# Float64 weights clamped on GpSimd one piece ahead, and VectorE's side work placed on other steps

## The chip, the cores and the metric

One core of a Trainium2 chip runs the whole kernel as one program. The metric is the device time of one execution in microseconds. Three executions of the kernel before took 1365.23, 1365.89 and 1360.34 us; their median is 1365.23 us. A profiled execution took 1369.21 us, of which the profile's span shows 1367.3 us.

## The reference

Three blocks follow each other. First attention of 8 batches and 8 heads over 576 positions of width 64, in two stages: 32 packed queries `p` attend to `k` and `v`, and then `q` attends to the packed result. Second a dense layer on the 4608 tokens (512 wide), whose weights are float64 in memory:

```python
h = x @ w_in            # 512 -> 2048
g = h - np.tanh(h)
x = (g @ w_out).astype(np.float32)   # 2048 -> 512
```

Third a mixture of 8 experts with one expert for each token, chosen by the largest gate logit: `out = gate_w * eom * (relu(x @ w1[e]) @ w2[e])`.

## The kernel before, in words

**The stages.** Stage A (context `pa`, 0 to about 128 us) packs `p` with `k` and `v` in 16 units `u` of one batch and four heads. The main stage (context `pb`, to about 860 us) does the second attention stage and the dense layer, and chooses the experts. Then come the experts. The change touches stage A and the main stage.

**Main stage.** The work goes in 16 halves `i`, each of half a batch (288 tokens, `HN`), numbered `(b, hf)`: an even half has `hf` = 0, an odd one 1. A half has 16 steps `f`, one for each 128 of the 2048 inner columns. Loop body number `m` issues, in this order: `up_b(m+1)`, `up(m+2)`, `down(m)`, at the last step of a half `drain`, and then what the table `todo` holds for this half and step, in the order in which `at` put it there. Each engine works in the order of issue.

- `up` (12 matmuls, L504 to L506) makes `ph` from the attention weights `a_hi`, `a_lo` of q and from the batch's fused weights `wf_hi`, `wf_lo`; ScalarE makes `th`, VectorE `gg = ph - th` (L510).
- `up_b` splits `gg`: ScalarE makes `gh` (L517), and `gl = gg - gh` (L518) is GpSimd's for the first `GP` = 12 steps of half 0 and VectorE's elsewhere.
- `down` (12 matmuls, L530 to L532) needs `gh` and `gl`, and adds to four accumulators in PSUM. Tiles `gg`, `gh`, `gl` and `ph` have two buffers each.
- `drain` copies the accumulators to `x2s` (one buffer), on ScalarE and VectorE (L540).

**The side work of the main stage**, put on steps by hand with `at`:

- `attend(i, fs, b, hf)`: the attention weights of one half. `load_q` (16 DMAs on SP into `qt`, two buffers) stands three steps before the first of `fs`; then `att_q` (VectorE transpose L175), `att_s` (16 matmuls L182 into two `px` banks), `att_f` (VectorE reads these), `att_x`, `att_n`, `att_t` (makes `a_hi`), `att_l` (makes `a_lo`). `up` of the next half's first step is issued in step 14.
- `weave(i, f, c, n)`: a quarter of the next batch's fused weights. `fuse` (16 matmuls L220 into two `px` banks) in step `f`, `fuse_h` (ScalarE) and `fuse_l` (VectorE `wf_lo`, L228, twice) in step `f` + 1.
- `make_z(n)`: 16 VectorE transposes of 32x32 (L159) of the next batch's packed result, in even halves. `fuse` and `att_s` read `z`.
- For the half before: `logits`, `logits_b`, `choose_a`, `choose_b`, `rank` (two matmuls into a `px` bank), `place` (VectorE, reads this bank at L597 and L601, then three indirect DMAs of GpSimd), `gate`, `gate_b` (VectorE, its multiply is L631; then four DMAs of `x2s` to DRAM on SP).

`px` is a pool of two PSUM banks that `att_s`, `fuse`, `logits`, `logits_b` and `rank` share.

**The conversion of the float64 weights.** `plan` lists 32 pieces of 128x512 numbers: 0 to 15 are of `w_in`, 16 to 31 of `w_out`. The first 20 (`NA`) are converted in stage A, one or two for each unit, and one in each of the steps 0 to 11 of half 0. `load_ahead(done)` keeps three pieces (`NST` buffers `st`) asked for on SP. `narrow` makes float32 out of a piece's two 32-bit words `hi` and `lo`: ScalarE takes the magnitude (L105), VectorE shifts and merges the bits (L107, L108, L109) and compares the magnitude with `TINY` (L110), and GpSimd multiplies by that mask (L113), which makes zeros of the smallest numbers. For `w_out`, `part_out` splits the piece one step later: ScalarE makes `hi` (L136), GpSimd `lo` (L137). In stage A a unit issues, near its end: `pack`'s reciprocal (L296, L297), the exponential (L277), `part_out` of the last unit's pieces, the conversion, and `load_ahead`.

## Time and profile before

| | us |
|---|---|
| median of three runs | 1365.23 |
| the profiled execution | 1369.21 |
| its span in the profile | 1367.3 |
| busy: TensorE, VectorE, ScalarE, GpSimd | 1265.3, 816.1, 530.1, 327.9 |

Busy times of the engines lie beside each other and don't add up to the span. In rows of the profile PE is TensorE (PEld its weight loads), DVE VectorE, ACT ScalarE, POOL GpSimd, SP the queue that issues most DMAs; L108 is line 108 of the kernel. A row of a timeline has the start in us from the span's start, the duration in us and the instruction; instructions of one line that follow each other are merged (x16), and in brackets stands the idle time of the engine before it and what ended it. Matmul ends are modelled.

### The profile page before, as it was taken

To read this page: it belongs to the slowest core of one execution; us is meant where nothing else is said; L and a number is where in the kernel's file an instruction comes from. 1 tells how busy PE (TensorE), PEld (TensorE's weight loads), DVE (VectorE), ACT (ScalarE), POOL (GpSimd) and SP (SyncE) were. 2 spreads that over 40 slices of the span, in tenths; PEclk is the share of its full clock that TensorE was granted. 3 is DMA by queue.
4 is the path that set the end of the run, shared out by engine and by line. 5 is a ranking of instruction groups with operands and counts; after the bars stand their busy time and mean duration, and the time that the engine had idled before them with its cause. 6 is when DMAs were issued, how large, how long until landed. Compare 5 with 4: busy or idle time off the path is not lost. (4 is left out here: it accounts for less than half of the span.)

```text
span 1367.3 us, 25742 instructions
## 1 busy us (share of the span) xinstructions
PE 1265.3 (93%) x9024; PEld 1082.4 (79%) x9024; DVE 816.1 (60%) x1811; ACT 530.1 (39%) x1141; POOL 327.9 (24%) x363
## 2 busy tenths in 40 slices
PE   6575879999999999999999999869999999999997
PEld 5354668998989989889899899757888778788775
DVE  3755996777776777768677777363233533443551
ACT  4555434443434344343434435332222422332431
POOL 3313760000000000000000000115444444454431
PEclk7878889999999999999999999989999999999999
DMA  8999421122111221122103023331113311332441
GB/s 227 242 246 207 138 64 22 15 36 36 27 19 27 36 30 24 19 36 36 26 11 53 19 47 112 117 80 39 44 47 101 105 46 45 113 100 73 131 154 41
DMA packets 140354, 102.24 MB, mean 75 GB/s; under 512 B 97296, under 2 KB 121876, under 8 KB 139572
## 3 DMA queue, kind: packets, MB, share of 16 engines
q1 hardware_dynamic: 130516, 80.33, 25.5%
q0 software_dynamic: 9696, 20.14, 4.8%
q8 instruction: 74, 1.21, 0.4%
q14 instruction: 68, 0.56, 0.2%
HBM read 215.60 MB, written 19.57 MB: 172 GB/s over the span
## 5 line engine op out<-in xcount | busy, mean ns | idle before, releaser
L610 POOL DMA_INDIRECT tab<-tok,ix x48 | 45.3, 943 | 641.5 <-DVE ix L608 460.7
L517 ACT ACTIVATE gh<-gg 128x288 fp32r<-128x288 f32 x256 | 112.6, 440 | 153.2 <-PE acc L532 68.0
L518 DVE TENSOR_TENSOR gl<-gg,gh 128x288 fp32r<-128x288 f32 x244 | 109.9, 450 | 96.9 <-ACT gh L517 90.6
L531 PE MATMUL acc<-gl,wo_bt 128*128 128x288 f32 x512 | 154.9, 303 | 11.5 <-DVE gl L518 7.0
L851 DVE TENSOR_TENSOR hl<-pt,hh 128x512 fp32r<-128x512 f32 x76 | 52.3, 690 | 185.4 <-ACT hh L850 174.2
L504 PE MATMUL ph<-a_hi,wf_hi 128*128 128x288 f32 x512 | 160.5, 314 | 0.9 <-DVE gg L510 0.5
L506 PE MATMUL ph<-a_hi,wf_lo 128*128 128x288 f32 x512 | 152.7, 298 | 3.9 <-DVE wf_lo L228 3.9
L531 PE MATMUL acc<-gl,wo_a 128*128 128x288 f32 x512 | 152.8, 298 | 3.7 <-POOL gl L518 3.7
L795 POOL DMA_INDIRECT xg<-x2d,iq x132 | 138.4, 1049 | 64.5 <-issue 57.0
L530 PE MATMUL acc<-gh,wo_a 128*128 128x288 f32 x512 | 152.1, 297 | 1.8 <-ACT pp L298 1.8
L532 PE MATMUL acc<-gh,wo_bt 128*128 128x288 f32 x512 | 152.8, 298 | 0.0
L530 PE MATMUL acc<-gh,wo_bt 128*128 128x288 f32 x512 | 152.7, 298 | 0.0
L505 PE MATMUL ph<-a_lo,wf_hi 128*128 128x288 f32 x512 | 152.3, 297 | 0.0
L532 PE MATMUL acc<-gh,wo_a 128*128 128x288 f32 x512 | 152.3, 297 | 0.0
L510 DVE TENSOR_TENSOR gg<-ph,th 128x288 f32<-128x288 f32 x256 | 115.9, 453 | 55.6 <-ACT th L508 54.3
L839 ACT ACTIVATE h<-ph 128x512 f32<-128x512 f32 x76 | 45.3, 598 | 241.1 <-PE ph L838 205.3
L508 ACT ACTIVATE th<-ph 128x288 f32<-128x288 f32 x256 | 104.1, 406 | 78.8 <-PE ph L506 77.7
L504 PEld LDWEIGHTS ph<-a_hi,wf_hi 128*128 128x128 f32 x512 | 97.3, 190 | 43.4 <-issue 38.6
L860 PE MATMUL py<-w2h,hh 128*128 128x512 f32 x304 | 127.0, 418 | 0.2
L861 PE MATMUL py<-w2l,hh 128*128 128x512 f32 x304 | 121.1, 398 | 1.7 <-DVE w2l L765 1.7
L837 PE MATMUL ph<-w1l,xh 128*128 128x512 f32 x304 | 121.2, 399 | 1.4 <-DVE w1l L765 1.0
L862 PE MATMUL py<-w2h,hl 128*128 128x512 f32 x304 | 120.8, 397 | 0.0
(223 smaller groups left out, 2756.8 us busy)
## 6 DMA issues: line engine op xcount, KB each, us to landing
raw<-in_moe_w_dram SPq DMA_DIRECT2D x37, 2048.0 KB
sraw<-in_moe_w_dram SPq DMA_DIRECT2D x37, 1024.0 KB
x2s<-in_moe_w_dram SPq DMA_DIRECT2D x37, 1024.0 KB
kt<-in_k_dram SPq DMA_DIRECT2D x16, 576.0 KB
vt<-in_v_dram SPq DMA_DIRECT2D x48, 192.0 KB
x2d<-x2s SPq DMA_DIRECT2D x64, 144.0 KB
qt<-in_q_dram SPq DMA_DIRECT2D x240, 36.0 KB
st<-in_moe_w_in_dram SPq DMA_DIRECT2D x16, 512.0 KB
```

The lines of the kernel that those rows point to most:

```text
L504: pe.matmul(ph, lhsT=wf_hi[n][:, g, c], rhs=ah[:, g], start=g == 0, stop=False)
L505: pe.matmul(ph, lhsT=wf_hi[n][:, g, c], rhs=al[:, g], start=False, stop=False)
L506: pe.matmul(ph, lhsT=wf_lo[n][:, g, c], rhs=ah[:, g], start=False, stop=g == 1)
L510: vec.tensor_tensor(gg, ph, th, op=ALU.subtract)
L530: pe.matmul(acc[j], lhsT=hi[:, j], rhs=gh, start=f == 0, stop=False)
L531: pe.matmul(acc[j], lhsT=hi[:, j], rhs=gl, start=False, stop=False)
L532: pe.matmul(acc[j], lhsT=lo[:, j], rhs=gh, start=False, stop=f == NF - 1)
L795: pool.indirect_dma_start(xg[:, g], None, src, bass.IndirectOffsetOnAxis(ap=iq[:, g:g + 1].bitcast(U32), axis=0))
L837: pe.matmul(ph, lhsT=xh[:, c], rhs=w1l[:, c, r], start=False, stop=False)
L860: pe.matmul(py, lhsT=hh[:, c], rhs=w2h[:, c], start=c == 0, stop=False)
L861: pe.matmul(py, lhsT=hh[:, c], rhs=w2l[:, c], start=False, stop=False)
L862: pe.matmul(py, lhsT=hl[:, c], rhs=w2h[:, c], start=False, stop=c == 7)
```

## The change

Conversion: the mask goes. `clamp` takes the magnitude of `hi` as float32 on ScalarE and raises it to at least `TINY` on GpSimd (one source, in place); VectorE's three bit operations then start from the clamped tile, and the last writes the result. `convert` clamps the next piece right after it has converted one, if that piece is asked for. `cvt` gets a third buffer. `lo` of `part_out` and the first 12 `gl` go from GpSimd to VectorE.

Main stage: `make_z` is cut by head over the steps 1, 3, 6 and 13. The even halves' `attend` ends in step 12 instead of 11; the odd halves' `att_q` goes from step 5 to 1 (with `load_q` from step 2 to step 14 of the half before). The fuses go from the steps 2, 5, 9, 14 to 3, 9, 11, 14. `rank`, `place`, `gate`, `gate_b` go from 4, 5, 5, 6 to 5, 6, 5, 7 in odd halves and to 4, 5, 6, 9 in even ones; halves 14 and 15 keep theirs.

```diff
--- before.py
+++ after.py
@@ -33,12 +33,11 @@
 NSTEP = NMAIN + NTAIL
 TROWS = NE * CAP + 128
 PAD = NT
-TINY = 1.125 * 2.0 ** -15
+TINY = 2.0 ** -15
 HF = NF // 2
 NST = 3
 UNITS = 2 * NB
 NA = 20
-GP = 12
 
 
 @with_exitstack
@@ -98,20 +97,34 @@
         return t[:, f % HF, 0], t[:, f % HF, 1]
 
 
-    def narrow(dst, st):
+    clamped = {}
+
+    def clamp(st):
+        t = cv.tile([128, 512], I32, name="cvt", bufs=3)
+        act.activation(t.bitcast(F32), st[:, :, 1].bitcast(F32), AF.Abs)
+        pool.tensor_scalar(t.bitcast(F32), t.bitcast(F32), TINY, None, op0=ALU.max)
+        return t
+
+    def narrow(dst, st, t):
         hi, lo = st[:, :, 1], st[:, :, 0]
-        top = st.rearrange("p n w -> p (n w)").bitcast(BF16).rearrange("p (n w) -> p n w", w=4)[:, :, 3]
-        mag = cv.tile([128, 512], BF16, name="mag")
-        act.activation(mag, top, AF.Abs)
-        t = cv.tile([128, 512], I32, name="cvt")
-        vec.tensor_scalar(t, hi, 0x07FFFFFF, 3, op0=ALU.bitwise_and, op1=ALU.logical_shift_left)
+        vec.tensor_scalar(t, t, 0x07FFFFFF, 3, op0=ALU.bitwise_and, op1=ALU.logical_shift_left)
         vec.scalar_tensor_tensor(t, lo, 29, t, op0=ALU.logical_shift_right, op1=ALU.bitwise_or)
-        vec.scalar_tensor_tensor(t, hi, -0x40000000, t, op0=ALU.bitwise_and, op1=ALU.bitwise_or)
-        vec.tensor_scalar(mag, mag, TINY, None, op0=ALU.is_ge)
-        src = t.bitcast(F32)
-        dst = src if dst is None else dst
-        pool.tensor_tensor(dst, src, mag, op=ALU.mult)
-        return dst
+        dst = t if dst is None else dst.bitcast(I32)
+        vec.scalar_tensor_tensor(dst, hi, -0x40000000, t, op0=ALU.bitwise_and, op1=ALU.bitwise_or)
+        return dst.bitcast(F32)
+
+    def clamp_next(i):
+        if i < len(plan) and i < ahead[0] and i not in clamped:
+            _, conv, n = plan[i]
+            st, w = (wst, w_out) if conv is conv_out else (ist, w_in)
+            if w.dtype != F32:
+                clamped[i] = clamp(st[n])
+
+    def convert(i):
+        _, conv, n = plan[i]
+        clamp_next(i)
+        conv(n, clamped.pop(i, None))
+        clamp_next(i + 1)
 
     wst, ist = {}, {}
 
@@ -124,17 +137,17 @@
             wst[f] = cv.tile([128, DM, 2], I32, name="st", bufs=NST)
             sp.dma_start(wst[f].rearrange("p n w -> p (n w)"), rows.bitcast(I32))
 
-    def conv_out(f):
+    def conv_out(f, t):
         wf = wst.pop(f)
         if w_out.dtype != F32:
-            wf = narrow(None, wf)
+            wf = narrow(None, wf, t)
         wst[f] = wf
 
     def part_out(f):
         sv = wst.pop(f).rearrange("p (g j d) -> p j g d", g=4, j=4)
         hi, lo = (x.rearrange("p j (g d) -> p j g d", g=4) for x in wo_of(f))
         act.activation(hi, sv, AF.Copy)
-        pool.tensor_tensor(lo, sv, hi, op=ALU.subtract)
+        vec.tensor_tensor(lo, sv, hi, op=ALU.subtract)
 
     def load_w_in(n):
         m, j = divmod(n, 4)
@@ -145,15 +158,17 @@
             ist[n] = cv.tile([128, 512, 2], I32, name="st", bufs=NST)
             sp.dma_start(ist[n].rearrange("p n w -> p (n w)"), w_in[rows, cols].bitcast(I32))
 
-    def conv_in(n):
+    def conv_in(n, t):
         m, j = divmod(n, 4)
         if w_in.dtype != F32:
-            narrow(w_in_sb[:, j, 512 * m:512 * m + 512], ist.pop(n))
-
-    def make_z(b):
-        z = z_t[b] = ef.tile([128, 4, 32], F32, name="zt", bufs=2)
+            narrow(w_in_sb[:, j, 512 * m:512 * m + 512], ist.pop(n), t)
+
+    def make_z(b, hs=range(4)):
+        if b not in z_t:
+            z_t[b] = ef.tile([128, 4, 32], F32, name="zt", bufs=2)
+        z = z_t[b]
         for g in range(2):
-            for h in range(4):
+            for h in hs:
                 for e in range(2):
                     r = 64 * (h % 2) + 32 * e
                     vec.transpose(z[r:r + 32, 2 * g + h // 2], pp[32 * h:32 * h + 32, 2 * b + g, 32 * e:32 * e + 32])
@@ -461,8 +476,8 @@
                 part_out(n)
             late = []
             want = (NA * u + LA - 2) // (LA - 1)
-            for _, conv, n in plan[done:want]:
-                conv(n)
+            for x, (_, conv, n) in enumerate(plan[done:want]):
+                convert(done + x)
                 if conv is conv_out:
                     late.append(n)
             done = want
@@ -515,7 +530,7 @@
             gh = gp.tile([128, HN], F32R, name="gh")
             gl = gp.tile([128, HN], F32R, name="gl")
             act.activation(gh, gg, AF.Copy)
-            (pool if (b, hf) == (0, 0) and f < GP else vec).tensor_tensor(gl, gg, gh, op=ALU.subtract)
+            vec.tensor_tensor(gl, gg, gh, op=ALU.subtract)
             g_t[b, hf, f] = gh, gl
 
         acc = {}
@@ -659,10 +674,11 @@
                 at(i, 1, logits_b)
                 at(i, 2, choose_a)
                 at(i, 3, choose_b)
-                at(i, 4, rank)
-                at(i, 5, place, *p_)
-                at(i, 5, gate, *p_)
-                at(i, 6, gate_b, *p_)
+                r, p_at, g_at, gb_at = (4, 5, 5, 6) if i >= 14 else (5, 6, 5, 7) if i % 2 else (4, 5, 6, 9)
+                at(i, r, rank)
+                at(i, p_at, place, *p_)
+                at(i, g_at, gate, *p_)
+                at(i, gb_at, gate_b, *p_)
             if i == 0:
                 weave(0, 0, 1, 0)
                 weave(0, 4, 2, 0)
@@ -676,7 +692,7 @@
                     part = []
                     take = plan[done:done + (2 if len(plan) - done > NF - 3 - f else 1)]
                     for x, (_, conv, m) in enumerate(take):
-                        at(0, f, conv, m)
+                        at(0, f, convert, done + x)
                         if conv is conv_out:
                             part.append(m)
                             assert f + 1 < m
@@ -688,15 +704,16 @@
             if n == NB:
                 continue
             if hf == 0:
-                attend(i, (4, 6, 7, 8, 9, 10, 11), b, 1)
-                at(i, 12, make_z, n)
+                attend(i, (4, 6, 7, 8, 10, 11, 12), b, 1)
+                for h, f in enumerate((1, 3, 6, 13)):
+                    at(i, f, make_z, n, (h,))
             else:
-                attend(i, (5, 7, 8, 9, 10, 11, 12), n, 0)
+                attend(i, (1, 7, 8, 9, 10, 11, 12), n, 0)
                 if n == NB - 1:
                     attend(i, (8, 12, 13, 14, 15, 16, 17), n, 1)
-                weave(i, 2, 0, n)
-                weave(i, 5, 1, n)
-                weave(i, 9, 2, n)
+                weave(i, 3, 0, n)
+                weave(i, 9, 1, n)
+                weave(i, 11, 2, n)
                 weave(i, 14, 3, n)
 
 
```

## Rows read from the trace of the kernel before

**Rows 1.** the page's first section, the whole span: busy time of each engine

```profile
PE 1265.3 (93%) x9024; PEld 1082.4 (79%) x9024; DVE 816.1 (60%) x1811; ACT 530.1 (39%) x1141; POOL 327.9 (24%) x363
```

**Rows 2.** windows: us of the stretch, then busy us (instructions) of each engine, PEclk, DMA share, GB/s

```profile
0.00:128.00 128.00, 81.63 (x1239) 60.00 (x1240) 66.67 (x161) 67.77 (x153) 32.65 (x60) 0.80 1.01 238
140.00:200.00 60.00, 46.37 (x294) 38.66 (x279) 59.00 (x84) 25.39 (x55) 42.86 (x35) 0.85 0.40 108
208.00:860.00 652.00, 644.03 (x5115) 585.84 (x5114) 471.66 (x1238) 272.88 (x667) 42.50 (x45) 1.00 0.20 33
```

**Rows 3.** waits of TensorE, the whole run: us in total, times, longest

```profile
PE pk L256 <- DMA kt<-in_k_dram: 28.1, 11, 6.5
```

**Rows 4.** groups by line and form, VectorE, 139.95 to 199.1 us: busy us, mean ns, idle

```profile
L108 DVE SCALAR_TENSOR_TENSOR cvt<-st,cvt 128x512 int32<-128x512 int32 x12 | 15.4, 1287 | 0.4
L109 DVE SCALAR_TENSOR_TENSOR cvt<-st,cvt 128x512 int32<-128x512 int32 x12 | 14.1, 1176 | 0.4
L107 DVE TENSOR_SCALAR cvt<-st 128x512 int32<-128x512 int32 x12 | 9.3, 774 | 0.0
...
L110 DVE TENSOR_SCALAR mag<-mag 128x512 bf16<-128x512 bf16 x13 | 4.8, 366 | 0.0
...
L518 DVE TENSOR_TENSOR gl<-gg,gh 128x288 fp32r<-128x288 f32 x2 | 0.9, 448 | 0.0
```

**Rows 5.** timeline, 149 to 156 us: start us, us, engine and instruction

```profile
151.03 1.72 POOL L137 TENSOR_TENSOR wo_a<-cvt,wo_a 128x512 fp32r<-128x512 f32 x1
...
151.65 1.65 DVE L109 SCALAR_TENSOR_TENSOR cvt<-st,cvt 128x512 int32<-128x512 int32 x1
```

**Rows 6.** timeline, VectorE, 108 to 124 us; idle time and its end in brackets

```profile
118.52 0.43 DVE L107 TENSOR_SCALAR cvt<-st 128x512 int32<-128x512 int32 x1 [3.83 <-DMA st<-in_moe_w_out_dram]
...
119.71 0.69 DVE L109 SCALAR_TENSOR_TENSOR cvt<-st,cvt 128x512 int32<-128x512 int32 x1
```

**Rows 7.** groups by line and form, whole run

```profile
L765 DVE TENSOR_TENSOR w1l<-raw,w1h 128x1024 fp32r<-128x1024 f32 x20 | 23.2, 1218 | 1.8 <-ACT w1h L764 1.8
...
L113 POOL TENSOR_TENSOR cvt<-cvt,mag 128x512 f32<-128x512 f32 x16 | 19.0, 1185 | 21.9 <-DVE mag L110 21.4 <-DVE rs L296 0.5
```

**Rows 8.** instructions of line 386: duration ns min/median/max, first and last start us

```profile
L386 POOL COPY scr<-scr x4: 396/494/595, 5.2 to 86.2; 128x256 f32<-128x256 f32 x4
```

**Rows 9.** timeline, TensorE, half 4 (to 384.96 us) and half 5

```profile
361.04 0.72 PE L182 MATMUL px<-qT,zt 64*32 64x288 f32 x16
...
379.33 0.29 PE L530 MATMUL acc<-gh,wo_bt 128*128 128x288 f32 x1
380.20 0.40 PE L531 MATMUL acc<-gl,wo_bt 128*128 128x288 f32 x1 [0.59 <-DVE gl L518]
...
382.56 0.30 PE L530 MATMUL acc<-gh,wo_bt 128*128 128x288 f32 x1
...
401.22 1.50 PE L220 MATMUL px<-w_in_sb,zt 64*32 64x512 f32 x16
...
403.56 0.30 PE L530 MATMUL acc<-gh,wo_a 128*128 128x288 f32 x1
...
405.94 0.29 PE L530 MATMUL acc<-gh,wo_a 128*128 128x288 f32 x1
...
408.03 1.31 PE L182 MATMUL px<-qT,zt 64*32 64x288 f32 x16 [0.33 <-DVE wf_lo L228]
...
414.24 1.09 PE L220 MATMUL px<-w_in_sb,zt 64*32 64x512 f32 x16
```

**Rows 10.** timeline, VectorE, halves 4 and 5

```profile
376.22 3.44 DVE L159 STREAM_TRANSPOSE zt<-pp 32x32 f32<-32x32 f32 x16
...
406.02 1.36 DVE L631 TENSOR_TENSOR x2s<-x2s,gw 128x1152 f32<-128x1152 f32 x1
407.29 1.28 DVE L228 TENSOR_TENSOR wf_lo<-px,wf_hi 128x512 fp32r<-128x512 f32 x2
```

**Rows 11.** timeline, ScalarE, 111 to 119 us

```profile
112.20 0.67 ACT L105 ACTIVATE mag<-st 128x512 bf16<-128x512 bf16 x1
```

## The prediction

> **What bounds the kernel now.** The page comes first: TensorE is busy for 93% of the span, VectorE for 60%, GpSimd for 24% [rows 1]. Averages over unlike stages, so the second view is a table by stage [rows 2]. It shows three regimes that the change touches. From 0 to 128 us (attention, `pa`) the DMA engines are full (share 1.01, 238 GB/s), and the longest wait of TensorE in the whole run is there, 28.1 us for k [rows 3]. From 140 to 200 us, half 0 of the main stage, VectorE is busy for 59.0 of 60 us and TensorE for 46.4, at a granted clock of 0.85 (a mix of the 1.2 and 2.4 GHz levels): VectorE bounds. From 208 to 860 us TensorE is busy for 644.0 of 652 us at clock 1.00 (2.4 GHz), so VectorE (471.7) costs only where something it owes comes late. After 860 us nothing is changed.
>
> **Half 0, the conversion.** Read the VectorE groups of its 12 pieces, plan numbers 20 to 31 [rows 4]: L107 0.774, L108 1.287, L109 1.176, L110 0.366, together 3.60 us a piece. The same instructions with GpSimd idle take 0.43 and 0.69 us [rows 6] (L108 like L109, both 128x512 with two sources). The surplus is waiting: L109 starts 0.62 us behind GpSimd's L137, which lasts 1.72, and takes 1.65 instead of 0.69 us [rows 5]. It ends about its own 0.69 us after GpSimd does.
>
> Removed per piece on VectorE: the four at 3.60. Added: three unheld, 0.43 + 0.69 + 0.69 = 1.81 (L107 now reads a plain tile; I take no gain for that). ScalarE's magnitude stays one instruction of 128x512, 0.67 [rows 11], off the bound. Added from GpSimd: `lo` of `part_out`, 128x512 with two SBUF sources, not in the trace on VectorE; bounds are half of the 1024-column subtract, 0.61 [rows 7], and L109's 0.69. I take 0.61, the same operation. And `gl` of the first 12 steps at 0.45 [rows 4]. Balance: 3.60 - 1.81 - 0.61 - 0.45 = 0.73 us a piece, 12 pieces, 8.8 us gained, before GpSimd's new clamp holds anything.
>
> The clamp, one source, 128x512: the nearest rows are a copy of 256 columns at 0.494 [rows 8], as a floor, and the two-source multiply of 512 columns that it replaces, 1.19 [rows 7], as a ceiling. Twice the copy is 0.99; less some fixed part I take 0.9. The Trainium skill, GPSIMD Engine Reference, Elementwise, counts about 1.8 cycles per element, 0.77 us here, and advises against GpSimd for an elementwise maximum; by 0.77 the held time below would be 4.6 and not 5.4 us. When does it hold VectorE? In a step ScalarE does `gh`, `th`, the `hi` of the previous piece and the next magnitude; VectorE meanwhile does `gl` and `gg`, then `lo` and the conversion. The clamp so arrives about when `lo` or L107 is running and takes its turn. In steps 1, 4, 5, 7, 8 and 9 of half 0 VectorE has pieces there that read PSUM or one tile (`fuse_l`, `att_q`, `att_f`, a reduction, ...), and the clamp runs beside them; in the other six it holds: 6 x 0.9 = 5.4 us. Ends: no step, 0; all twelve at 1.19, 14.3. Half 0 thus gains 3.4 us, between -5.5 and +8.8.
>
> **Stage A and its seam.** The clamp takes L110 off VectorE, which there waits on ScalarE, but loads bound that stage, so I count nothing. Against it: the magnitude is now computed one piece earlier, and ScalarE works in order. The magnitude of piece 15 ended at 112.87, and the next one would stand there, while VectorE's L107 shows that piece 16 landed only at 118.52 [rows 6, 11]. ScalarE would be held 5.6 us with the copies of the next attention unit behind it. Cover: TensorE's 28.1 us of waits for k, which lie in the same stage. At the seam VectorE loses the wait on the magnitude in front of the last unit's reciprocal, and gets four `lo` that wait for `hi`: about even. I take 0, between -3 and +3.
>
> **Main stage, odd halves.** A bare step is 2.38 us (403.56 to 405.94). Two bursts on the `px` banks are stretched [rows 9]. The fuse of step 5 lasts 1.50 against 1.09 of a free one, because its second bank is still `rank`'s until `place` has read it: 0.41. `att_s` in step 7 lasts 1.31 against 0.72 in the even half, and idles 0.33 in front: 0.92. The VectorE rows say why: `gate_b`'s 1.36 us multiply stands ahead of the two `wf_lo` that free the banks [rows 10]. The change moves the fuse of step 5 to 9, and `att_s` of 7 finds the banks long free. Both waits go, 1.33 us. But the fuse of step 9 moves to 11, and its predecessor's `wf_lo` stands in step 10 behind `att_n`, the same figure as step 6 today: one large piece, then `wf_lo`, then a burst one step on. I charge 0.92 for it, between 0 and 1.33. Net 0.41 a half, 7 halves: 2.9 us.
>
> In half 13 the second `attend` is left where it was, so its `att_s` stands in step 12 ahead of the `wf_lo` for the fuse of step 11, whose banks it needs. Nearest row 0.92; more here, as `att_l` is ahead too: 1.3, once.
>
> **Even halves.** `make_z`, 3.44 us in one piece at step 12 [rows 10], delays `gl`: TensorE idles 0.59 in step 14, and the step lasts 3.23 instead of 2.38 [rows 9], 0.85 lost. Six halves have it: 5.1 us. Spread by head, a quarter is 0.86 us, and steps 1, 3, 6, 13 have room. What is late next: `gate_b` now falls in step 9, between `att_x` and `att_n`, and `a_lo` moves from 11 to 12, two steps before the first use. By adding up VectorE's queue, `gl` of steps 12 and 13 comes late by a few tenths. I leave 0.3 of the 0.85, between 0 and 0.85: gain 6 x 0.55 = 3.3 us.
>
> **Moved at no cost.** `load_q` of the odd halves, 16 DMAs on SP, goes from step 2 to step 14 of the half before; it follows `gate_b`'s four writes on SP (then at step 9), and `att_q` comes three steps later; two `qt` buffers cover it. Gone, `att_q` would wait, with `gl` behind it. `gate_b`'s writes at 9 and 7 instead of 6 still leave six steps before `drain` needs their tile. `place` a step later moves three indirect DMAs on GpSimd, which is otherwise idle there (42.5 of 652 us) [rows 2].
>
> **Sum.** 3.4 + 0 + 2.9 - 1.3 + 3.3 = 8.3 us. The profiled execution took 1369.2 us and would take 1360.9; the median of the runs, 1365.2, is 4.0 lower, so I forecast 1357.
>
> **The rivals.** (1) *The lock takes back half 0.* If each clamp holds VectorE, 12 x 0.9 = 10.8 eats the 8.8. For it: L107, L108 and L109 are all held today [rows 4 to 6], and `lo` and `gl` read two tiles as L109 does; against it, half of the steps have other work there. If the even halves also keep their wait in a new place, 2.9 - 1.3 - 2.0 are left: no gain, 1365. The Trainium skill, SBUF — State Buffer, Who interferes with whom, states it as a rule: the two engines share a port pair as an exclusive lock, and a VectorE instruction with two SBUF inputs waits in full behind a GpSimd one that reads SBUF. By that rule this rival holds wherever the two meet; the pair of rows agrees, but does not say how often they will. (2) *All goes.* The clamp never meets a held instruction and no new wait appears: 8.8 + 7 x 1.33 + 5.1 = 23.2, 1342. For it: VectorE has 180 us idle between 208 and 860. Against it: `fuse_l` one step before a fuse. (3) *Slower: ScalarE waits for weights.* It stands at each early magnitude. Piece 16 would cost 5.6; if four such places exist (the pieces after a step with two of them are the same case) it is 22 us. TensorE's idle time on k absorbs these unless they delay the release of k and v buffers and so the loads. It decides once some 15 us come through: 22 - 8.3 gives 1379. (4) *It does not do what it says*: a clamp is skipped when its piece is not yet asked for. Three are asked for ahead, so that hardly happens.
>
> **How the numbers follow.** A measurement of this kernel tells about 0.5% from no change, 6.8 us. The forecast has 0.47, rival 1 0.24, rival 2 0.18, rival 3 0.09, rival 4 0.02. Below 1358.4 lie two thirds of the forecast's cases (0.31), all of rival 2 and a quarter of rival 1: 0.55. Slower by that much: most of rival 3 and a little of 1 and 4: 0.10. The rest, 0.35, is the same. The range reaches half-way into rival 2, 1345, and over rival 1 with its seam, 1367.
>
> **What would show it.** L107 to L109 at a mean near 0.5, 0.8 and 0.8 us in half 0, `gl` and `lo` on VectorE; half 0 some 3 us shorter. No wait of L182 for `wf_lo` but one of L220; step 14 of the even halves near 2.7 us. ScalarE's magnitude idle in front near 113 us. I am wrong if half 0 isn't shorter, if the fuse of step 11 is not stretched, or if the main stage begins over 3 us away from where it does now.

## The result and the profile after

Nine executions of the changed kernel took 1344.68 to 1356.67 us, median 1348.39; nine of the kernel before, beside them, had a median of 1363.94. The ratio is 0.9887, 95% interval 0.987 to 0.9905: 15.4 us faster, where 8.3 were forecast. 1348.4 lies inside the range given; the forecast, 1357, is 8.6 us above it.

The profiled execution took 1347.29 us, its span is 1345.3. The page's busy times, to hold against [rows 1]:

```profile
PE 1256.2 (93%) x9024; PEld 1078.5 (80%) x9024; DVE 803.5 (60%) x1807; ACT 531.9 (40%) x1141; POOL 313.7 (23%) x335
```

The same three regimes as in [rows 2], by windows (columns as there):

```profile
0.00:128.00 128.00, 85.67 (x1254) 61.59 (x1255) 62.77 (x146) 69.18 (x159) 40.67 (x61) 0.76 0.95 241
137.00:197.00 60.00, 47.64 (x306) 39.46 (x305) 53.87 (x106) 27.34 (x58) 18.16 (x11) 0.81 0.41 108
203.00:855.00 652.00, 645.16 (x5160) 591.74 (x5159) 476.41 (x1245) 278.59 (x674) 52.60 (x51) 1.00 0.21 34
```

In half 0 VectorE is busy for 53.9 of 60 us where it was for 59.0: it no longer fills the stretch. TensorE's granted clock is 0.81 there, a mix of its two levels. From 203 to 855 us TensorE has 6.8 us left idle of 652.

TensorE's waits in the whole run (us in total, times, longest) answer to [rows 3]. The wait for k went from 28.1 to 17.5 us. The second row is half 0, the third is the first matmul of the main stage's down projection (the one wait of half 13 that the prediction named stands under e6):

```profile
PE pk L271 <- DMA kt<-in_k_dram: 17.5, 8, 3.7
...
PE ph L521 <- DVE wf_lo L243: 4.3, 2, 2.7
PE acc L545 <- ACT pp L313: 3.0, 1, 3.0
```

The VectorE groups of half 0, 137 to 197 us (busy us, mean ns), answer to [rows 4]; L110, L111 and L113 are the three that are left of a conversion, L150 is `lo`:

```profile
L111 DVE SCALAR_TENSOR_TENSOR cvt<-st,cvt 128x512 int32<-128x512 int32 x12 | 9.9, 821 | 0.4
L113 DVE SCALAR_TENSOR_TENSOR cvt<-st,cvt 128x512 int32<-128x512 int32 x13 | 9.0, 692 | 0.4
L110 DVE TENSOR_SCALAR cvt<-cvt 128x512 int32<-128x512 int32 x12 | 6.1, 509 | 0.4 <-POOL cvt L105 0.4
...
L150 DVE TENSOR_TENSOR wo_bt<-cvt,wo_bt 128x512 fp32r<-128x512 f32 x7 | 4.8, 683 | 2.5 <-ACT wo_bt L149 2.5
```

Over the whole of half 0, from 137 to 208 us before and from 134 to 203 us after (columns as in [rows 2]), VectorE's work fell by 7.7 us, and its idle time rose from 2.7 to 8.4 us:

```profile
137.00:208.00 71.00, 55.83 (x352) 46.97 (x351) 68.27 (x109) 31.75 (x70) 45.73 (x38) 0.86 0.35 96
```

```profile
134.00:203.00 69.00, 55.39 (x352) 47.03 (x353) 60.56 (x120) 31.72 (x69) 19.91 (x12) 0.82 0.38 101
```

VectorE's longest waits in it, before and then after (us in total, times, longest), are for ScalarE, which makes `gh` and the `hi` of a piece:

```profile
DVE gl L518 <- ACT gh L517: 1.1, 2, 0.6
```

```profile
DVE gl L533 <- ACT gh L532: 3.4, 3, 2.2
DVE wo_bt L150 <- ACT wo_bt L149: 2.5, 2, 1.3
```

To place the difference I cut each trace at the first matmul of the down projection in each half (L530 before, L545 after); every figure below is the distance of two such starts (the first row counts from the span's start, the last to its end).

| us | before | after | e1: places alone | e2: conversion alone | e3: fuse at 12 |
|---|---|---|---|---|---|
| start of the main stage | 136.65 | 133.92 | 141.91 | 134.18 | 135.99 |
| half 0 | 71.38 | 69.08 | 71.37 | 71.34 | 70.49 |
| an odd half (half 5) | 46.89 | 45.61 | 45.61 | 46.90 | 45.30 |
| an even half (half 6) | 41.35 | 40.69 | 40.69 | 41.36 | 40.71 |
| half 13 | 47.69 | 48.15 | 48.23 | 47.64 | 48.15 |
| halves 1 to 13 | 578.1 | 566.0 | 566.1 | 577.2 | 564.2 |
| half 14 to the end | 581.1 | 576.3 | 572.5 | 576.0 | 576.0 |

Halves 1 to 13 repeat to 0.1 us from kernel to kernel where their code is the same (two of before's had a disturbance of 0.4 and 0.5). The first rows and the last do not: the code from half 14 on is the same in all (but for e6, whose last attention steps reach into half 14), and takes 572.5 to 581.5 us in the twenty profiles of this study. So a pair of profiles tells the steps of halves 1 to 13, and nothing under some 5 us elsewhere; there only several profiles, or the times, do. Before's profiled execution is such a case: it is long at its end, and above all its runs.

### The profile page after: what moved, and what is told of

The parts are those of the page before. It is cut to its first block, busy times and chain, and to the rows that moved or that the text cites. A ratio compares the mean times of both kernels' runs of the same rounds, so it can differ in the third digit from the quotient of the medians.

```text
span 1345.3 us, 25723 instructions
## 1 busy us (share of the span) xinstructions
PE 1256.2 (93%) x9024; PEld 1078.5 (80%) x9024; DVE 803.5 (60%) x1807; ACT 531.9 (40%) x1141; POOL 313.7 (23%) x335
## 5 line engine op out<-in xcount | busy, mean ns | idle before, releaser
L625 POOL DMA_INDIRECT tab<-tok,ix x48 | 52.1, 1086 | 629.6 <-DVE ix L623 470.2
L533 DVE TENSOR_TENSOR gl<-gg,gh 128x288 fp32r<-128x288 f32 x256 | 115.9, 453 | 82.9 <-ACT gh L532 80.8
L545 PE MATMUL acc<-gh,wo_a 128*128 128x288 f32 x512 | 152.1, 297 | 4.3 <-ACT pp L313 3.0
L545 PE MATMUL acc<-gh,wo_bt 128*128 128x288 f32 x512 | 152.5, 298 | 0.7 <-ACT gh L532 0.7
## 6 DMA issues: line engine op xcount, KB each, us to landing
kt<-in_k_dram SPq DMA_DIRECT2D x16, 576.0 KB
```

Of the source, the lines that this page charges most:

```text
L545: pe.matmul(acc[j], lhsT=hi[:, j], rhs=gh, start=f == 0, stop=False)
```

## Experiments

Each kernel ran beside the kernel before. Ratios are to that, so 0.9887 is the changed kernel's; in brackets stands the 95% interval.

### The two parts by themselves

**e1_steps_only**: the kernel before, with the diff's places of the steps in the main stage and its `make_z` by heads, and nothing else.

> This is the kernel of before with the new places of the steps alone (the weaves, the attend of the odd halves, rank, place and gate, and the reshape of z cut in four); the conversion, the float32 subtraction of lo and gl stay as they were. Theory A (the gain of the main stage comes from the places of the steps): halves 1 to 13 of the main stage get 12 us shorter in sum (578 to 566 us: odd halves 46.9 to 45.6, even ones 41.4 to 40.7), the main stage starts where it did (136.7 +- 1), half 0 stays at 71.4 +- 1, and the whole is 12 us (10 to 13) under the kernel of before. Theory B (the faster halves come from buffers or engines that the new conversion frees, so that the places alone bring little): halves 1 to 13 gain under 6 us and the whole under 7 us. A clear middle (7 to 10 us) would say that the two parts help each other.

Median 1354.41, ratio 0.9925 (0.9897 to 0.9952), 10 us. Halves 1 to 13 came to 566.1 as theory A had it, and not to the 572 or more of B; 0.9 of the 12.0 us are the two disturbances of before's profile, so the places bring 11. "The start where it was" missed: 141.9, with the very code of before.

**e2_conv_only**: the changed kernel with the old places.

> This is the changed kernel with the old places of the steps in the main stage: the new conversion (clamp on GpSimd one piece ahead), lo and gl on VectorE are all that differs from the kernel of before. Theory A (the conversion's part is the start of the main stage and half 0 alone): main starts 2.7 us earlier (133.9), half 0 is 2.3 us shorter (69.1), halves 1 to 13 stay at 578 +- 1.5, the whole 4 to 6 us under the kernel of before. Theory B (the prediction's term for half 0 was right and the seam brings nothing): half 0 is 3.4 us shorter, the start unchanged. Theory C (the conversion brings nothing, since GpSimd holds VectorE): the whole within 1.5 us of before. With e1_steps_only the two parts should add to the whole change, -15 to -17 us; a sum that misses it by over 3 us would say that they help or hinder each other.

Median 1358.19, ratio 0.9960 (0.9945 to 0.9975), 5.4 us, the size of A. But half 0 took 71.34, as before. So A's split is wrong in half 0; together 1.15% against 1.13% of the whole change: the parts add.

### What the clamp on GpSimd holds

**e4_clamp_vec**: the max of the clamp on VectorE.

```diff
-        pool.tensor_scalar(t.bitcast(F32), t.bitcast(F32), TINY, None, op0=ALU.max)
+        vec.tensor_scalar(t.bitcast(F32), t.bitcast(F32), TINY, None, op0=ALU.max)
```

> The changed kernel with the max of the clamp on VectorE in place of GpSimd; nothing else differs, and the result stays the same. Theory A (GpSimd's one-source max stretches VectorE by some 0.3 us where they meet, not by its own 1.48 us): VectorE saves about 0.3 a piece and pays the max itself, some 0.4 to 0.5 a piece, so half 0 (12 pieces) is 1 to 2 us longer or unchanged, the start of main within 1 us, the whole 0 to 4 us above the changed kernel. Theory B (the max holds VectorE for its whole 1.48 us): VectorE saves about 1 us for each piece, half 0 is 5 to 9 us shorter where VectorE is its bound, and the whole 4 to 8 us under the changed kernel. Theory C (half 0 is no longer bound by VectorE but by the weights that land late): within 1 us either way, with the waits of ScalarE for the weights as they were.

Ratio 0.9897 (0.9872 to 0.9923), level with the change; half 0 68.95. Theory B is out; A and C are not told apart. The main stage started at 139.4, where A had it within 1 us of the changed kernel's 133.9. The groups of VectorE in half 0, as above, of this kernel:

```profile
L113 DVE SCALAR_TENSOR_TENSOR cvt<-st,cvt 128x512 int32<-128x512 int32 x13 | 9.0, 692 | 0.4
L111 DVE SCALAR_TENSOR_TENSOR cvt<-st,cvt 128x512 int32<-128x512 int32 x12 | 8.3, 692 | 0.4
...
L110 DVE TENSOR_SCALAR cvt<-cvt 128x512 int32<-128x512 int32 x12 | 5.1, 422 | 0.0
L105 DVE TENSOR_SCALAR cvt<-cvt 128x512 f32<-128x512 f32 x12 | 5.0, 420 | 1.3 <-ACT cvt L104 1.3
```

With GpSimd silent L110 takes 0.422 and L111 0.692 us; with the clamp there, 0.509 and 0.821. The clamp so holds VectorE by 0.09 + 0.13 = 0.22 us a piece, 2.6 us in half 0. The max costs VectorE 0.42 us and GpSimd 1.49 (line 105 of the changed kernel, ns min/median/max):

```profile
L105 POOL TENSOR_SCALAR cvt<-cvt x32: 1476/1488/2012, 22.9 to 187.1; 128x512 f32<-128x512 f32 x32
```

**e8_no_ahead**: the clamp just ahead of its own conversion.

```diff
         conv(n, clamped.pop(i, None))
-        clamp_next(i + 1)
```

> The changed kernel with the clamp of a piece issued just ahead of its own conversion, not one piece ahead; nothing else differs. Theory A (without the piece ahead VectorE waits at each conversion for ScalarE's Abs and GpSimd's max: 0.67 and 1.49 us and two hand-overs): some 2 us for each of 12 conversions in half 0, less what VectorE has idle there (7.6 us of 66), so half 0 is 10 to 18 us longer (79 to 87), the stage before it 0 to 4 us longer, the whole 10 to 20 us above the changed kernel, slower than before the change. Theory B (VectorE's idle time and the weights' landing take the wait in): half 0 within 3 us and the whole within 4 us.

Median 1362.17, ratio 0.9974 (0.9953 to 0.9994): all but 3.6 of the change's 15.4 us are gone, about 12. Half 0 took 77.2 us and the main stage started at 143.7; both grew, the start more than A had it, half 0 less. VectorE's waits for the clamp, up to the start of main and then in half 0, say where; in the changed kernel this wait is 0.4 us in half 0:

```profile
DVE cvt L110 <- POOL cvt L105: 50.9, 16, 10.0
```

```profile
DVE cvt L110 <- POOL cvt L105: 11.2, 11, 1.5
```

The lookahead is what makes a slow GpSimd instruction cheap: without it the new conversion is some 7 us slower than the old one (e1, 0.9925).

**e7_lo_gpsimd** and **e11_gl_gpsimd**: one VectorE instruction each back on GpSimd, `lo` of every piece and `gl` of the first twelve steps.

```diff
-        vec.tensor_tensor(lo, sv, hi, op=ALU.subtract)
+        pool.tensor_tensor(lo, sv, hi, op=ALU.subtract)
```
```diff
-            vec.tensor_tensor(gl, gg, gh, op=ALU.subtract)
+            (pool if (b, hf) == (0, 0) and f < 12 else vec).tensor_tensor(gl, gg, gh, op=ALU.subtract)
```

> The changed kernel with the subtraction that makes lo of w_out back on GpSimd. Theory A (taking lo off GpSimd is what makes the start of the main stage earlier: GpSimd did 1.2 us for the subtraction and 1.2 for the multiply of each piece in a row): main starts up to 2.7 us later again, half 0 changes by less than 1 us since VectorE does not bound it any more, the whole 0 to 3 us above the changed kernel. Theory B (VectorE bounds half 0): VectorE saves 0.68 us for each of nine pieces, half 0 is 3 to 6 us shorter. Theory C (GpSimd's two-source subtraction holds VectorE for its whole 1.2 us): half 0 is 3 to 6 us longer.

> The changed kernel with gl of the first twelve steps of half 0 back on GpSimd, where the kernel of before had it. VectorE is rid of twelve instructions of 0.45 us (5.4 us), and GpSimd, which was 20 us busy in half 0, does them in some 0.8 to 1.0 us each, between the clamps. Theory A (VectorE's queue does not bound half 0 by its sum but by what stands in it when a chain needs it; the longer gl stands on the path of the down projection): half 0 within 1.5 us of the five profiles of the same conversion (69.1 to 71.3), the whole within 2 us of the changed kernel. Theory B (half 0 is bound by VectorE's sum): half 0 is 3 to 5 us shorter and the whole as much under the changed kernel. Theory C (gl behind the clamps of 1.5 us on GpSimd is late): half 0 is 3 to 8 us longer.

Ratios 0.9858 (0.9828 to 0.9888) and 0.9867 (0.9838 to 0.9896); half 0 68.6 and 71.6. Against a mean of 70.2 in five profiles with the new conversion (69.08, 71.34, 70.49, 69.44, 70.86), neither is the 3 to 6 us of the theories in which VectorE's sum bounds half 0. But neither run tests these theories, for VectorE's sum hardly fell: over half 0 it is busy for 60.1 us in e7 and 61.0 in e11, against 60.6 in the changed kernel. What moved to GpSimd came back as longer instructions on VectorE. In e7, 142 to 202 us:

```profile
L111 DVE SCALAR_TENSOR_TENSOR cvt<-st,cvt 128x512 int32<-128x512 int32 x13 | 13.4, 1029 | 0.4
L113 DVE SCALAR_TENSOR_TENSOR cvt<-st,cvt 128x512 int32<-128x512 int32 x13 | 10.6, 812 | 0.4
```

In the changed kernel these take 821 and 692 ns. In the times neither move can be told from none. The main stage started at 139.1 in e7, 5 us later than in the changed kernel where A allowed 2.7, and at 129.0 in e11.

### The steps

**e3_fuse12**: the third fuse of the odd halves one step later.

```diff
-                weave(i, 11, 2, n)
+                weave(i, 11 if n == NB - 1 else 12, 2, n)
```

> The changed kernel with the third fuse of the odd halves one step later (12 in place of 11; in half 13 it stays at 11). In the changed kernel the step that begins with this fuse takes 3.92 us where the other steps with a fuse take 3.58 to 3.61, and the fuse's matmuls write where wf_lo of the second fuse (step 10) has just been read. Theory A (the 0.33 us is TensorE's wait for VectorE's wf_lo of step 10, drawn as a longer matmul): at step 12 it falls to 3.58 to 3.62, the odd halves 1 to 11 get 0.3 us shorter each (45.6 to 45.3), 2 us in sum, the whole 1.5 to 2.5 us under the changed kernel, hard to tell in the times and plain in the step lengths. Theory B (the wait moves on to where wf of step 14 needs wf_lo of step 13, or to att_n and att_t, which lie in steps 10 to 12): the odd halves stay at 45.6 +- 0.1 and another step is longer by 0.3.

Ratio 0.9862 (0.9834 to 0.9891). Odd halves 1 to 11 took 45.30 each, 0.31 less, as theory A; no other step grew. First half 5 of the changed kernel, TensorE (step 11 begins at 406.55 and step 12 with the fourth row; its fuse is the third row):

```profile
396.64 0.72 PE L197 MATMUL px<-qT,zt 64*32 64x288 f32 x16
...
402.25 1.09 PE L235 MATMUL px<-w_in_sb,zt 64*32 64x512 f32 x16
...
408.24 1.40 PE L235 MATMUL px<-w_in_sb,zt 64*32 64x512 f32 x16
...
410.46 0.29 PE L545 MATMUL acc<-gh,wo_bt 128*128 128x288 f32 x1
```

and VectorE there, `att_n`'s last piece and the `wf_lo` behind it:

```profile
406.54 0.76 DVE L218 TENSOR_TENSOR ex<-ex,asm 128x576 f32<-128x576 f32 x1
407.21 1.28 DVE L243 TENSOR_TENSOR wf_lo<-px,wf_hi 128x512 fp32r<-128x512 f32 x2
```

In e3 the same fuse, in step 12, takes what a free one does:

```profile
411.84 0.30 PE L545 MATMUL acc<-gh,wo_bt 128*128 128x288 f32 x1
...
413.51 1.09 PE L235 MATMUL px<-w_in_sb,zt 64*32 64x512 f32 x16
...
415.43 0.29 PE L545 MATMUL acc<-gh,wo_bt 128*128 128x288 f32 x1
```

**e6_h13**: half 13's second attend a step later from `att_s` on.

```diff
-                    attend(i, (8, 12, 13, 14, 15, 16, 17), n, 1)
+                    attend(i, (8, 13, 14, 15, 16, 17, 18), n, 1)
```

> The changed kernel with the second attend of half 13 one step later from att_s on (8, 13 to 18 in place of 8, 12 to 17). In the changed kernel half 13 takes 48.15 us where the other odd halves take 45.61, with one step of 4.82 us in which TensorE waits 0.94 us for wf_lo of step 12. Theory A (that wait comes from the weave at 11 and the att_s at 12 that share the two buffers of PSUM): 0.9 to 1.6 us shorter, half 13 at 46.5 to 47.2. Theory B (half 13 is longer by the matmuls of its second attend alone): half 13 within 0.3 us of 48.15, a wait of another kind in another step. In both, half 14 (41.83) may get 0.3 us longer, since the end of the second attend falls into it.

Ratio 0.9889 (0.9858 to 0.9921). Half 13 fell to 46.85, in A's bounds, but half 14 rose from 41.83 to 43.01: 0.1 us in all. In the changed kernel, then in e6:

```profile
758.50 1.31 PE L197 MATMUL px<-qT,zt 64*32 64x288 f32 x16 [0.94 <-DVE wf_lo L243]
```

```profile
757.85 0.71 PE L197 MATMUL px<-qT,zt 64*32 64x288 f32 x16
...
769.42 0.69 PE L562 MATMUL px<-x2s,wgt 128*32 128x288 f32 x8 [2.00 <-DVE wf_lo L243]
```

`att_s` is free in e6, and the next half's first step waits 2.00 us for the last `wf_lo` instead. The 1.2 us moved by one half.

### The start of the main stage

**e5_q_split**: q's 16 transfers of step 1 spread over steps 0 to 2, behind each step's load of weights.

```diff
-                attend(0, (4, 6, 7, 8, 9, 10, 11), 0, 1)
+                for f, fn in zip((4, 6, 7, 8, 9, 10, 11), (att_q, att_s, att_f, att_x, att_n, att_t, att_l)):
+                    at(0, f, fn, 0, 1)
...
+                    for j in ((0, 1), (2,), (3,))[f] if f < 3 else ():
+                        at(0, f, load_q, 0, 1, (j,))
```

> The changed kernel with the 16 transfers of q that half 0 issues in step 1 spread over steps 0, 1 and 2, each behind that step's load of the weights; nothing else differs. Theory A (in half 0 ScalarE waits 3.7 us and 1.9 us for weights that were issued behind q's transfers, and what is queued behind it on ScalarE and VectorE ends the step): those waits fall below 2 us in sum, half 0 gets 1.5 to 4 us shorter (69.1 to 65 to 67.5), the rest is unchanged, the whole 1.5 to 4 us under the changed kernel. Theory B (the wait is covered, since the matmuls of half 0 wait for gl and wf_lo on VectorE anyway): the waits of ScalarE shrink, the time stays within 1 us. Theory C (q's own arrival then ends a step, in step 4 where it is first read): slower by up to 3 us, with a new wait on q's tile.

Ratio 0.9889 (0.9867 to 0.9911), half 0 70.7: no gain. ScalarE's waits for weights in half 0 fell from 5.6 us (longest 3.7) to 3.6 (1.8), not below 2, and a new one of 2.3 us stands on VectorE, for q and behind a load of weights: theory C's wait, with B's result.

```profile
DVE qT L190 <- DMA st<-in_moe_w_out_dram: 2.3, 1, 2.3
```

**e10_pack15**: the last unit's division and copy one unit earlier, ahead of the last conversions.

```diff
-            if 1 < u < UNITS + 2:
+            if 1 < u < UNITS + 1:
                 pack(u - 2)
+            if u == UNITS:
+                pack(u - 1)
```

> The changed kernel with the last unit's division and copy (the sum's reciprocal on VectorE, the copy on ScalarE) issued one unit earlier, ahead of two conversions and their subtraction of lo, so that they no longer stand behind these on VectorE and ScalarE. Theory A (the main stage's first matmuls of the down projection wait 3.0 us for that copy, and nothing else is late there): main starts 2 to 3 us earlier than in the same code without it (131.3 to 136.0 in five profiles, so 129 to 133), some 1 us of it is lost again in half 0, since the conversions come later, and the whole is 1 to 3 us under the changed kernel. Theory B (the wait only moves to the weights that these conversions make): the first matmul waits as long for lo or for gl, half 0 grows by what the start gains, the whole within 1 us. Theory C (the matmuls of the last unit then stand ahead of other work on TensorE and hold it): slower by up to 3 us.

Ratio 0.9887 (0.9859 to 0.9916): theory B. TensorE's waits from 129.5 to 142 us of it:

```profile
PE ph L521 <- ACT wf_hi L239: 4.3, 1, 4.3
...
PE acc L547 <- ACT pp L313: 0.4, 1, 0.4
```

The 3.0 us for `pp` fell to 0.4; the stage started at 129.6, half 0 took 74.6, and step 1 now waits 4.3 us for `wf_hi`.

**e12_best**: e3 and e10 together, and the last part of `make_z` later.

```diff
-                for h, f in enumerate((1, 3, 6, 13)):
+                for h, f in enumerate((1, 3, 6, 15)):
```

> Three edits of the changed kernel together, which act in different stretches: the third fuse of the odd halves at step 12 (as in e3_fuse12), the last unit's division and copy one unit earlier (as in e10_pack15), and the last part of z's reshape in the even halves at step 15 in place of 13. Theory A: the odd halves 1 to 11 take 45.3 us; the even ones 40.4 to 40.6, since the step that began behind the reshape took 2.60 to 2.62 us where its neighbours take 2.38 to 2.40, so 1.2 us in sum; the start of the main stage as in e10_pack15; in all 3 to 6 us under the changed kernel, 1343 to 1346. Theory B (the reshape at 15 delays gl of the next half's first step, where the drain stands): the even halves stay at 40.7 or get 0.2 longer with step 15 or the odd halves' step 0 longer, and the whole is 1 to 3 us under the changed kernel.

Ratio 0.9857 (0.983 to 0.9884). Odd halves 45.30; even ones 40.71, as theory B had them: step 13 still takes 2.62 us. The whole is level with e3's 0.9862. The rows that tell why are in the changed kernel's half 4: on VectorE `gl` waits 1.08 us for ScalarE's `gh`, and `make_z`'s quarter (L174) comes later; on ScalarE `gh` stands behind `a_hi`, the copy of the transpose `aT`:

```profile
367.95 0.46 DVE L533 TENSOR_TENSOR gl<-gg,gh 128x288 fp32r<-128x288 f32 x1 [1.08 <-ACT gh L532]
...
370.21 0.87 DVE L174 STREAM_TRANSPOSE zt<-pp 32x32 f32<-32x32 f32 x4
```

```profile
366.90 0.69 ACT L224 ACTIVATE a_hi<-aT 128x576 fp32r<-128x576 f32 x1 [2.58 <-DVE aT L222]
367.50 0.43 ACT L532 ACTIVATE gh<-gg 128x288 fp32r<-128x288 f32 x1
```

**e9_hold_loads**: e1 with the weights' loads two pieces ahead instead of three in the stage before main. It asked whether the new conversion starts main earlier by holding the weights' loads back.

```diff
-            load_ahead(done)
+            load_ahead(done - 1)
```

> The kernel of e1_steps_only (the old conversion, the new places) with the loads of the float64 weights two pieces ahead of the conversion in place of three in the stage before the main one; nothing else differs. In that stage the new conversion holds the queue of SP some 25 us for pieces that are not yet converted, the old one 5 us, and the same 31.5 MB arrive at 241 to 251 GB/s in place of 231 to 238. Theory A (the main stage starts earlier because the weights' loads are held back and the loads of k and v get through): main starts at 133 to 137 in place of 136.7 and 141.9 (old conversion), TensorE's wait for k falls from 28 to 33 us to about 20, and the whole is 2 to 5 us under e1_steps_only (1354.4). Theory B (the start is earlier because each piece is converted with less work on VectorE and GpSimd): main starts where it did in the two kernels with the old conversion, 136 to 142, or later, half 0 is 0 to 3 us longer since its weights land later, and the whole 0 to 4 us above e1_steps_only.

Ratio 0.9873 (0.9843 to 0.9903) against e1's 0.9925: it looked like theory A, though main started at 138.0. It was measured beside other runs, so the four combinations went onto one chip, all with e3's fuse: **f1_old**, **f2_old_hold**, **f3_new** (the kernel of e3 again), **f4_new_hold**.

> First of four kernels with the same main stage from half 1 on (the new places, the third fuse at step 12), run on one chip: the old conversion, weights loaded three pieces ahead. Both theories: halves 1 to 13 at 564 us, main starts at 137 to 142, half 0 at 71.4, the whole 12 to 14 us under the kernel of before. Theory A (loads held back): the slowest of the four or level with f4, 3 to 5 us above f2 and f3. Theory B (less work in the conversion): level with f2 within 1.5 us, and 4 to 5 us above f3 and f4.

> Second of four: the old conversion, weights loaded two pieces ahead in the stage before the main one. Theory A (the loads held back let k and v through): main starts 3 to 5 us earlier than in f1, TensorE's wait for k 20 to 23 us in place of 28 to 33, the whole 3 to 5 us under f1 and within 2 us of f3. Theory B (less work in the conversion makes the gain): within 1.5 us of f1, 4 to 5 us above f3.

> Third of four: the new conversion (clamp on GpSimd one piece ahead, lo and gl on VectorE), weights loaded three pieces ahead; the same kernel as e3_fuse12. Both theories: main starts at 131 to 136, half 0 at 69 to 71.3, the whole 16 to 19 us under the kernel of before. Against f1, 4 to 5 us shorter in both; against f2, level by theory A, 4 to 5 us shorter by theory B.

> Fourth of four: the new conversion, weights loaded two pieces ahead in the stage before the main one. By theory A (holding loads is what helps, and the new conversion already does it by SP's waits for it) a second hold brings nothing: within 1.5 us of f3, or slower by up to 4 us, as ScalarE and VectorE then wait for pieces not yet landed. By theory B it changes nothing either unless pieces come late; a gain of over 2 us against f3 would say that the two act each by itself and add up.

| | median us | ratio (95%) | start of main | half 0 |
|---|---|---|---|---|
| f1 old | 1351.32 | 0.9879 (0.9858 to 0.9900) | 142.5 | 71.35 |
| f2 old, hold | 1351.49 | 0.9887 (0.9866 to 0.9907) | 137.5 | 71.35 |
| f3 new | 1346.79 | 0.9845 (0.9825 to 0.9865) | 133.7 | 70.86 |
| f4 new, hold | 1350.99 | 0.9885 (0.9852 to 0.9918) | 135.0 | 69.32 |

Theory A falls: f1 and f2 are level, f3 is 4.5 us under f1, near what e2 gave. f4 is 4.2 us above f3, with intervals that overlap. It is no clean test: with loads two pieces ahead, the next piece is not yet asked for behind the second of two pieces in one unit, and its clamp then comes late (twice in that stage). f3 and e3 are one kernel, with 0.9845 and 0.9862; e7 (0.9858) and e12 (0.9857) can't be told from it. Against the changed kernel's 0.987 to 0.9905 e3's interval overlaps and f3's ends just below; the step lengths say 1.9 us. TensorE's waits up to 130 us in f1, then in f2, show why a wait's size is not its price: 11.4 us less for k, 13.3 new ones for ScalarE's copy of it.

```profile
PE pk L258 <- DMA kt<-in_k_dram: 36.0, 13, 5.9
```

```profile
PE pk L258 <- DMA kt<-in_k_dram: 24.6, 10, 5.3
PE pk L287 <- ACT kT L259: 13.3, 6, 5.2
```

The last thing that the main stage waits for is the last unit's reciprocal (L298, L299), which stands on VectorE behind the conversion. In f1, VectorE:

```profile
133.67 0.91 DVE L110 TENSOR_SCALAR mag<-mag 128x512 bf16<-128x512 bf16 x1 [4.15 <-ACT mag L105]
...
140.88 0.90 DVE L110 TENSOR_SCALAR mag<-mag 128x512 bf16<-128x512 bf16 x1 [1.24 <-ACT mag L105]
141.70 0.14 DVE L298 TENSOR_SCALAR rs<-rs 128x1 f32<-128x1 f32 x1
```

The mask L110 waits 4.15 and 1.24 us for ScalarE's magnitude, the reciprocal stands behind it, and the main stage begins at 142.5. In the changed kernel `lo` (L150) waits 2.05 and 0.48 us for ScalarE in that stretch, and no mask stands ahead of the two reciprocals' first halves (L311):

```profile
128.11 0.14 DVE L311 TENSOR_SCALAR rs<-rs 128x1 f32<-128x1 f32 x1
...
133.12 0.15 DVE L311 TENSOR_SCALAR rs<-rs 128x1 f32<-128x1 f32 x1
```

**f5_old_ahead**: f1 with the magnitude alone one piece ahead, by the diff's `clamp_next` and `convert`.

> The kernel of f1_old with ScalarE's magnitude issued one piece ahead, as the change does with its clamp; the mask, the multiply on GpSimd, lo and gl stay as in the kernel of before. Theory A (what the new conversion brings at the start of the main stage is that VectorE no longer stands in front of its mask for ScalarE): VectorE's waits for the magnitude in the last 40 us before the main stage fall from 9 to 14 us to under 3, main starts at 133 to 137 in place of 136.7 to 142.5, half 0 stays at 71.4 +- 1, the whole 3 to 5 us under f1_old's 1351.3, ratio to before 0.984 to 0.986. Theory B (the gain comes from the lighter work: no mask and multiply, lo off GpSimd): main starts at 137 to 142, the whole within 1.5 us of f1_old, ratio 0.987 to 0.989.

Ratio 0.9870 (0.9844 to 0.9895), by the ratio at the lower edge of B's bounds; its median is 2.4 us under f1's, between the theories. In the last 40 us before main, f1's VectorE had this wait, and f5's has none for the magnitude; its longest is for TensorE:

```profile
DVE mag L110 <- ACT mag L105: 9.2, 3, 4.2
```

```profile
DVE mx L290 <- PE sc L286: 9.3, 3, 4.6
```

Main started at 132.8, A's size; half 0 71.6. The profile is for A, the times can't tell it from B.

**g_na18**: f3 with two pieces moved from that stage into half 0.

```diff
-NA = 20
+NA = 18
```

> The kernel of f3_new with 18 in place of 20 pieces of weights converted ahead of the main stage, so 14 in place of 12 in half 0. Two pieces are 1.05 MB of the 31.5 MB that arrive before main starts. Theory A (the stage before is bound by its bytes, at 235 to 240 GB/s, and half 0 by VectorE's pieces): main starts 4.4 us sooner than in f3_new and the same code elsewhere (131.3 to 136.0, mean 133.4), so at 127 to 131, half 0 gets 4 to 8 us longer (69.1 to 71.3 before; two pieces of some 2.7 us of VectorE each, less its idle time), the whole 0 to 4 us above f3_new. Theory B (half 0 has room on VectorE, 58 of 66 us busy): half 0 is longer by less than 3 us, and the whole 1 to 4 us under f3_new, the shortest of all. Theory C (the stage is bound by its engines and not by bytes): main starts where it did, half 0 is longer, the whole 4 to 8 us above f3_new.

Ratio 0.9908 (0.9881 to 0.9936), 6 us above f3. Main started at 133.0, not sooner, and half 0 took 75.2: theory C. By this one profile the stage is not bound by bytes at its end: A had asked for a start at 127 to 131.

## Why the prediction was right and wrong

**Right**: faster; both parts count; the mean durations asked for in half 0, near 0.5, 0.8 and 0.8 us, are 0.51, 0.82 and 0.69; the two stretched bursts of the odd halves and the wait behind `make_z` are gone; ScalarE does stand for weights in that stage, as rival 3 had it, and the main stage started earlier all the same. ScalarE's waits up to 130 us:

```profile
ACT cvt L104 <- DMA st<-in_moe_w_in_dram: 12.2, 3, 5.8
```

**The step that failed** is "But the fuse of step 9 moves to 11", with "I charge 0.92 for it, between 0 and 1.33. Net 0.41 a half, 7 halves: 2.9 us". The charge measured 0.31 (step 11 takes 3.92 us, a free fuse's step 3.61; e3). I had taken `att_n` for the same figure as `gate_b`. It isn't: the piece ahead of `wf_lo` is 0.76 us and not 1.36 [rows 10], `wf_lo` begins 0.66 us into the step of the burst instead of 1.35, and 0.69 earlier is about what the charge was too high. The gain was a little more than 1.33 as well: 0.42 in step 5, 1.00 in step 7, and 0.17 in step 13, which I had not looked at. An odd half gained 1.59 - 0.31 = 1.28, six of them 7.7 us. Half 13 cost 0.46 against before (-1.3 + 0.41 was forecast, so 0.9).

**Even halves**: 0.55 forecast, 0.67 measured, 4.0 us over six. Step 14 takes 2.38 us where it took 3.23 [rows 9]. The few tenths left over are there (step 13, 2.60 us), by ScalarE's order and not by VectorE's queue. The steps 13, 14 and 15 of half 4 begin so:

```profile
368.23 0.29 PE L545 MATMUL acc<-gh,wo_bt 128*128 128x288 f32 x1
...
370.83 0.30 PE L545 MATMUL acc<-gh,wo_bt 128*128 128x288 f32 x1
...
373.21 0.29 PE L545 MATMUL acc<-gh,wo_bt 128*128 128x288 f32 x1
```

**Half 0 and the seam** had the wrong shares. The hold, charged 5.4 us, is 2.6 by e4, and VectorE lost 7.7 us of work in half 0, more than the 3.4 forecast. The step that failed here is the one from work to time, "VectorE bounds": five profiles of half 0 with the new conversion average 70.2 against 71.4 in each with the old one, 1.1 us, not 3.4. The rest became idle time of VectorE, 8.4 us where it was 2.7, most of it waits for ScalarE's `gh` and `hi`. What bounds half 0 now is not shown. And the seam, taken as 0 between -3 and +3, is where the rest seems to lie: starts of 133.9, 134.2, 136.0, 131.4 and 133.7 (mean 133.8) against 136.7, 141.9 and 142.5. I had named the reciprocal's wait and set `lo`'s wait for `hi` against it as "about even"; by these starts it isn't, though e4 and e7, which keep the lookahead, started at 139.4 and 139.1. From the times (e2, f3 against f1) start and half 0 are worth 4.5 to 5.4 us together; the profiles would say 7 to 8, within their scatter. That the new conversion needs the lookahead is shown by e8, in its time and its waits. Whether the lookahead at the magnitude or the lighter work makes the earlier start stays open: in f5's profile VectorE's wait is gone and the start is early, but its times can't be told from f1's.

**The sum**: 7.7 - 0.5 + 4.0 = 11.2 from the places, some 5 from the conversion, 16 us; measured 15.4. Against the forecast the odd halves with half 13 bring 5.6 us more, the even ones 0.7, the conversion 1 to 2.

**The rivals**. Rival 1's hold of every meeting in full is not there. The Trainium skill, SBUF — State Buffer, Who interferes with whom, makes such a VectorE instruction wait until GpSimd's is through. The trace does not agree: L111, with two SBUF inputs, ends at 127.22 while the clamp, as drawn (spans on GpSimd are rough), runs to 127.54, and is 0.29 us longer than alone:

```profile
125.78 1.76 POOL L105 TENSOR_SCALAR cvt<-cvt 128x512 f32<-128x512 f32 x1 [1.86 <-ACT cvt L104]
...
126.24 0.98 DVE L111 SCALAR_TENSOR_TENSOR cvt<-st,cvt 128x512 int32<-128x512 int32 x1
```

By that rule half 0 could have had twelve waits of up to 1.5 us; e4 puts the hold at 2.6 in all, and the measurement decides. In [rows 5] too L109 ended 0.55 us after GpSimd's instruction, less than its own 0.69, so the pair agreed with a wait in full only roughly. Rival 2, in which all goes, would have had 7 x 1.33 + 5.1 = 14.4 us from the places; 11.2 came, for the fuse in step 11 still costs 0.31 a half, half 13 lost 0.5 and the even halves keep a few tenths. Rival 3's price was never asked. Rival 4 is out: by the order in which the code asks for pieces, every next one has been asked for when its clamp is due.

## What to carry to other kernels

A stretched burst is priced from the instruction that really stands ahead of its releaser, not from a neighbour that looks alike: 0.6 us there, six times, was about half of this miss. A slow engine's instruction costs its latency only where someone waits for it; one piece of lookahead was worth about 12 us here, and which engine did the max made no difference that the times show (e4). Moving a subtraction of two tiles from VectorE to GpSimd freed nothing on VectorE, whose other instructions took about as much longer beside it (e7). Where one wait of a serial start is taken away (k, `pp`, q's transfers, half 13's `att_s`), look for the next one before counting a gain: four of these experiments shortened a wait and left the time.

## What was not expected of the hardware

GpSimd's max of 128x512 with one source takes 1.49 us, above the 1.19 of the two-source multiply it replaced [rows 7], and outside the bounds 0.49 to 1.19 that I gave; VectorE does it in 0.42. The Trainium skill, GPSIMD Engine Reference, Elementwise, gives 0.77 us for 512 columns as its best case; the trace does not come near it. A stage whose DMA share is 0.95 was not shortened by 1.05 MB less (g_na18, one profile). Beside GpSimd's two-source subtraction L111 took 1.03 us on the mean, beside the one-source max alone 0.82, and 0.69 with GpSimd silent (e7, the changed kernel, e4).
